# A new order of one block, new bank tables and a new list for the first blocks, in a fused causal convolution and SiLU MLP kernel

## The chip, the cores and the metric

The kernel runs on one core of one Trainium2 chip. The metric is the device time of one execution in microseconds (us); lower is better. Everything is float32.

## What is computed

A causal convolution over the sequence, with 7 taps per head that a softmax makes from `weight`, and behind it an MLP with SiLU:

```python
x_unf = x_pad[:, idx, :].reshape(B, S, K, H, group)   # B, S, D = 8, 4096, 192; K = 7, H = 8
out = np.einsum('hk,bskhg->bshg', softmax(weight), x_unf)
x = out.reshape(B * S, D)                             # 32768 tokens
h = x @ w_in                                          # 192 -> 2048
g = h * (1.0 / (1.0 + np.exp(-h)))
return g @ w_out                                      # 2048 -> 192
```

## The kernel before

The 32768 tokens are cut into 32 blocks of 1024, each in two parts of 512 tokens. Both matrix products are done with a fast scheme (as Strassen's and Winograd's): fewer products, and more sums of operands and of results around them. A block goes through these steps, each named by a short token in the kernel's text:

- **Convolution of the block to come.** `ld.k` loads x for channels k (k = 0, 1, 2) with 4 transfers on the sync queue (SP). `i.k` transposes it on VectorE. `v.ki` does tap i: tap 0 is a scaled copy on ScalarE into `nat`; taps 1 to 6 are done on VectorE (L516) for the first blocks, and from block 4 on are a scaled copy on ScalarE (L511) into a buffer `u`, and a transfer on GpSimd's queue (POOL) that adds it to `nat` (L512). `sp.k` spreads the result into `dup` on the SP queue (11 transfers a block, L533), `w.i` builds five sums of it (`win`, L550 and L553) on VectorE. `ha.0` fetches the 6 tokens from before the block.
- **Up phase** (tokens `P`, `L`; L649 and L666). `Pr.g` is product r (0 to 14) of group g (0 to 4): one matmul of 64 rows by 128 columns against 512 tokens. 64 rows are half of the TensorE array: a product is on rows 64 to 127 when r is in `ON_B` and (g, r) is not `SWAP`, otherwise on rows 0 to 63. The two halves can work at the same time. `L.0k` is one such matmul on rows 0 to 63, and `L.1k` one of 256 columns on each half. Products of one chain (`CHAINS`) add up in one PSUM bank. A block has 75 products P and 6 L: 40.5 full matmuls for each half.
- **Sums and SiLU of the results**: `u` copies a chain's bank to SBUF (ScalarE, L698), `X`, `a` and `b` add chains (VectorE, L692), `S` and `SL` apply SiLU (ScalarE, L710 and L715) into `g`. A product of another group can use a bank only when these have read it.
- **Output phase**: `t.ji` makes sums of `g` on VectorE (L733). `Di.je` (out_slot, L765) is four matmuls of 32 columns each, side by side in the array; 48 of them a block, 8 with 128 tokens (D5) and 40 with 512. They add up in the banks of `ACC`.
- **Results**: `x`, `y`, `z` copies (ScalarE), `M1` to `M7` sums (VectorE), `o.k` transposes, `st.k` stores 3 transfers each on the SP queue.

What order this runs in is written out by hand. `PLAN` is one string of tokens, and it is done once for each block b; a token with `-` ahead of it works on block b - 1, with `=` on b - 2, with `+` on b + 1. So one pass of the list does the output phase of the block before, while the convolution of the next is prepared, and then the up phase of block b; the list is a ring, and its last products are followed by the first tokens of the next pass (before: `... P8.2 b1.3 P4.3 P14.3`, and then `P5.0 -a1.3 -P10.2 ...`). `START` is a list of the same kind for the first blocks; in it `=dp` is a step of the plain second product of block 0 (`down_plain`, L786), whose banks are `DOWN_BANKS`, and `go.2` and combinations on GpSimd prepare the weights. Every instruction of the list is pinned to the program's order on its engine: each engine works its own queue in the order of the tokens, and waits on semaphores for the others.

The tables `CHAIN_BANKS`, `XBANKS`, `PLAIN_BANKS` and `ACC` say which of the 8 PSUM banks each chain and sum uses, one row for block 1, one for block 2 and one for all later blocks.

The end (`finish`) does the last block's second half and stores it.

Of the kernel before, what the change touches and what calls it, by code (L numbers as in the profile page):

```python
# [17 lines left out]
def kernel(  # L18
# [60 lines left out]


    PLAN = (
# [20 lines left out]
    )  # L102
    START = (
# [40 lines left out]
    )  # L144
    QUEUE = (0, 4, 1, 2, 3)
    CHAIN_BANKS = (
# [3 lines left out]
    )  # L150
    XBANKS = (
# [3 lines left out]
    )  # L155
    PLAIN_BANKS = (
        (0, 2, 3),
        (2, 2, 1),
        (6, 5, 7),
    )  # L160
    ACC = (
        (3, 2, 5, 6, 7, 1, 0),
        (4, 6, 3, 5, 1, 7, 0),
        (4, 7, 5, 1, 3, 6, 0),
    )

    def pin(ins):
        return tc.keep_in_program_order(ins)
# [37 lines left out]
    x0 = x.flatten_outer_dims()[TB - pad : TB, :].rearrange("t (k c) -> c k t", k=NK)  # L206
# [565 lines left out]
                )  # L772
            )

    DOWN_BANKS = (7, 4, 2)

    def down_plain(b):

        cmbs[b] = [xpool.tile([P, 4, TB], F32, tag="cmb", name="cmb")]
        for j in range(NJ):  # L780
            for a in range(2):
                for e in range(2):
                    for k in range(NK):
                        for n in range(2):
                            pin(
                                nc.tensor.matmul(  # L786
                                    banks[DOWN_BANKS[k]][R * n : R * n + R, :],
                                    wo[j][:, a, e, R * k : R * k + R],
# [14 lines left out]
    def copy_plain(b, k):  # L803
        pin(nc.scalar.copy(cmbs[b][0][:, k, :], banks[DOWN_BANKS[k]]))

# [329 lines left out]
```

## Time and profile before

| | us |
|---|---|
| runs of the kernel | 2368.7, 2369.21, 2367.38 |
| their median | 2368.7 |
| the profiled execution's own time | 2367.17 |
| its span (first to last instruction) | 2365.1 |

| part of the span | us |
|---|---|
| until the output phase of block 2 begins | 218.60 |
| 28 blocks of the planned order, to the output phase that begins at | 2250.14 |
| from there to the end | 114.96 |

How to read the profile: an engine's busy time is the time in which at least one of its instructions runs. PE is TensorE's matmuls, PEld its weight loads, DVE VectorE, ACT ScalarE, POOL GpSimd, SP the sync engine, and a q behind a name is its queue of transfers. Two matmuls on the two halves of the array overlap, and count once. The end of a matmul is modelled; its start is measured, so distances between starts are what can be trusted. L765 is line 765 of the kernel. The mean granted clock of TensorE is 0.999, so the clock was not held back.

Instructions of a group with their mean length (ns): a product (L649) is listed as two matmuls, one for each of the two passes in which a float32 matmul is done, of 589 to 595 each; the sums of L692 take 684 to 692 and those of L733 1219 to 1224; a copy of L698 587, SiLU 597 to 629, a scaled copy of L511 717.

### The profile page before, as it was taken

What the parts mean: (1) busy time and instruction counts of PE and PEld (TensorE: products, weight loads), DVE (VectorE), ACT (ScalarE), POOL (GpSimd) and SP (SyncE); (2) the same over time, 40 slices, a digit from 0 to 9 for tenths busy, and PEclk for the clock granted to TensorE, in tenths of its full rate; (3) what the DMA queues carried; (4) which work ended last, traced back from release to release, by engine and by line L of the source; (5) the groups of instructions that cost most, each with busy time, mean ns of one, the idle gap of its engine ahead of it and who ended that gap; (6) DMA issues with size and microseconds to landing.
All of it is one profiled execution on the core that took longest, in us unless ns stands there. A gap on an engine that the chain in (4) does not pass through costs nothing.

```text
span 2365.1 us, 45608 instructions
## 1 busy us (share of the span) xinstructions
PE 2352.3 (99%) x17630; PEld 1156.1 (49%) x17630; DVE 1797.8 (76%) x2373; ACT 1503.1 (64%) x2779; POOL 530.3 (22%) x672
## 2 busy tenths in 40 slices
PE   9999999999999999999999999999999999999998
PEld 5345544455544555444555445554445544455544
DVE  8898777787777777777877777777777777787776
ACT  5247666677666686666766666766667666677643
POOL 4921122211222111222122221212211122212100
PEclk9999999999999999999999999999999999999999
DMA  7324567665566655766656766556666567655510
GB/s 157 70 48 82 87 116 120 108 104 102 100 117 120 107 104 90 120 120 105 106 97 104 120 112 106 104 92 116 121 110 109 88 113 120 111 103 97 90 29 14
DMA packets 523833, 238.81 MB, mean 101 GB/s; under 512 B 431648, under 2 KB 436768, under 8 KB 523616
## 3 DMA queue, kind: packets, MB, share of 16 engines
q0 software_dynamic: 73024, 133.73, 33.4%
q1 hardware_dynamic: 447392, 101.78, 24.1%
q8 instruction: 138, 2.26, 0.4%
q10 hardware_dynamic: 3200, 0.39, 0.1%
q14 instruction: 79, 0.65, 0.1%
HBM read 31.46 MB, written 25.17 MB: 24 GB/s over the span
## 4 chain that ended last, share of the span: by engine, by line
PE 97%; DVE 2%; issue 0%; SPq 0%; ACT 0%; DMA 0%; DVEq 0%; ACTq 0%
PE ps L765 47%; PE ps L649 45%; PE ps L666 2%; PE ps L588 2%; DVE nat L516 1%; PE ps L1034 1%; DVE two L175 0%; DVE g L692 0%; PE ps L435 0%; DVE mh L175 0%; SPq L533 0%; DVE xt L477 0%; DVE t L733 0%; DMA dup<-nat 0%; DVE ps L692 0%
## 5 line engine op out<-in xcount | busy, mean ns | idle before, releaser
L512 POOL DMA_DIRECT2D nat<-u x504 | 431.7, 943 | 1586.4 <-DMA out_dram<-osb 716.0
L765 PE MATMUL ps<-g,wo 128*32 128x512 f32 x2976 | 681.1, 593 | 0.0
L649 PE MATMUL ps<-win,wr 64*128 64x512 f32 x1550 | 648.2, 594 | 0.0
L649 PE MATMUL ps<-win,ws 64*128 64x512 f32 x1550 | 617.7, 595 | 0.2 <-DVE ps L692 0.2
L698 ACT COPY u<-ps 128x512 f32<-128x512 f32 x775 | 444.0, 587 | 135.3 <-PE ps L649 115.5
L765 PE MATMUL ps<-t,wo 128*32 128x512 f32 (+1 forms) x4528 | 523.5, 446 | 0.0
L765 PE MATMUL ps<-t,wx 128*32 128x512 f32 x2976 | 475.1, 592 | 0.6 <-DVE t L733 0.6
L649 PE MATMUL ps<-dup,wr 64*128 64x512 f32 x868 | 442.6, 591 | 4.6 <-DVE ps L692 4.6
L692 DVE TENSOR_TENSOR g<-u,ps 128x512 f32<-128x512 f32 x465 | 315.3, 684 | 92.8 <-PE ps L649 63.4
L733 DVE TENSOR_TENSOR t<-g,t 128x1024 f32<-128x1024 f32 x248 | 303.4, 1224 | 105.6 <-PE ps L765 98.2
L710 ACT ACTIVATE g<-g 128x512 f32<-128x512 f32 x465 | 279.7, 629 | 139.9 <-DVE g L692 139.7
L733 DVE TENSOR_TENSOR t<-g 128x1024 f32<-128x1024 f32 x248 | 302.1, 1219 | 63.8 <-PE ps L765 58.1
L511 ACT ACTIVATE u<-xt,taps 128x512 f32<-128x512 f32 x504 | 341.7, 717 | 1.5
L649 PEld LDWEIGHTS ps<-win,wr 64*128 64x128 f32 x1550 | 262.8, 187 | 154.4 <-issue 71.3
L710 ACT ACTIVATE g<-ps 128x512 f32<-128x512 f32 x465 | 268.1, 597 | 73.7 <-PE ps L649 71.8
L649 PEld LDWEIGHTS ps<-win,ws 64*128 64x128 f32 x1550 | 264.6, 187 | 99.0 <-issue 34.3
L765 PEld LDWEIGHTS ps<-t,wo 128*32 128x32 f32 x4528 | 180.1, 110 | 220.3 <-issue 209.7
L649 PE MATMUL ps<-dup,ws 64*128 64x512 f32 x682 | 273.2, 594 | 0.0
L823 ACT COPY yx<-ps 32x128 f32<-32x128 f32 x120 | 30.8, 257 | 364.5 <-PE ps L765 363.1
L765 PEld LDWEIGHTS ps<-t,wx 128*32 128x32 f32 x2976 | 121.7, 110 | 278.4 <-issue 250.6
L765 PE MATMUL ps<-g,wx 128*32 128x512 f32 x1488 | 245.3, 592 | 0.0
L692 DVE TENSOR_TENSOR ps<-u,ps 128x512 f32<-128x512 f32 x310 | 214.3, 692 | 39.9 <-PE ps L649 24.3
(92 smaller groups left out, 2041.8 us busy)
## 6 DMA issues: line engine op xcount, KB each, us to landing
nat<-u POOLq DMA_DIRECT2D x504, 256.0 KB, 4.2
dup<-nat SPq DMA_DIRECT2D x345, 128.0 KB, 2.4
nat<-in_x_dram SPq DMA_DIRECT2D x382, 64.0 KB, 4.1
out_dram<-osb SPq DMA_DIRECT2D x376, 64.0 KB, 2.2
raw<-in_moe_w_out_dram SPq DMA_DIRECT2D x8, 384.0 KB, 3.7
raw<-in_moe_w_in_dram SPq DMA_DIRECT2D x12, 192.0 KB, 4.5
ws<-wr POOLq DMA_DIRECT2D x8, 192.0 KB, 4.9
raw<-in_moe_w_in_dram SPq DMA_DIRECT2D x6, 128.0 KB, 3.2
```

The lines of the kernel that those rows point to most:

```text
L511: pin(nc.scalar.activation(z, src, AF.Copy, scale=tap))
L512: pin(nc.gpsimd.dma_start(out=dst, in_=z, accum_op=ALU.add))
L516: nc.vector.scalar_tensor_tensor(out=dst, in0=src, scalar=tap, in1=dst, op0=ALU.mult, op1=ALU.add)
L588: nc.tensor.matmul(hs[a, n, e], rows(wr[j], e)[:, a, k, :], rows(d, e)[:, n, k, :], start=k == 0, stop=k == NK - 1,)
L649: nc.tensor.matmul(to[:, cols], raw(g, *LEFT[e][r], e), rhs[:, cols], start=first, stop=True, skip_group_check=True,)
L666: nc.tensor.matmul(plain_bank(b, n and 1 + e)[:, cols], rows(wr[j] if own == e else ws[j], e)[:, a, k, :], rows(dups[b], e)[:, SLOT[e][2 * ...
L692: pin(nc.vector.tensor_tensor(out_, u, v, op=op))
L698: pin(nc.scalar.copy(us[b, g, o][:, cols], t1[:, cols]))
L710: pin(nc.scalar.activation(h, src, AF.Silu))
L733: pin(nc.vector.tensor_tensor(t[i // 2][:, i % 2, :], u, v, op=ALU.subtract))
L765: nc.tensor.matmul(accs[b][at][SQ * q : SQ * q + SQ, to], lhs[:, e, SQ * k : SQ * k + SQ], rhs[:, e, ts(q, TB // 4) if i == 5 else to], st ...
L823: nc.scalar.copy(to[:, ts(q, TB // 4)], acc[5][SQ * q : SQ * q + SQ, 0 : TB // 4])
```

## The change

The lists PLAN and START and the tables of banks are replaced; no other line is changed but the banks of `down_plain`. The tokens of PLAN are the same ones, each once, in another order, and some are done one pass earlier or later (another sign). The functions that they call are the same. In START all steps `=dp` come ahead of the first product. Of START, the diff shows the lines that matter below.

```diff
     PLAN = (
-        "P5.0 -a1.3 -P10.2 -a0.2 -P10.3 -b5.3 -P8.3 -S4.3 -sp.0 -D0.31 -S0.1 -S1.0 -D1.10 v.20 "
-        "-S3.3 -D1.30 -S1.4 -D1.21 -D0.00 -t.00 -t.01 -D2.00 -D2.01 =st.1 v.11 -t.03 -D4.01 "
-        "-S1.1 -t.10 -D4.00 -D5.00 v.00 v.01 -D0.10 -sp.2 -t.11 -D2.10 -D1.01 v.12 -b5.2 v.02 "
-        "-t.13 -D5.10 -D4.10 -t.12 -D3.10 -D4.11 -S5.2 v.21 -w.0 -t.02 -D3.00 v.03 -D2.11 v.13 "
-        "-D3.01 -D1.11 -D5.11 -w.1 -D5.01 +ld.2 -D1.31 v.14 v.04 -D0.11 -D3.11 -D1.20 -a0.3 "
-        "v.15 u5.0 -S1.2 -S0.2 -t.20 -D0.20 -t.21 -D2.21 -t.22 -S0.3 -D2.20 -w.2 v.22 -S1.3 "
-        "+ld.1 -S5.3 -t.23 -D4.20 -D4.21 -D5.21 -D5.20 -D3.20 v.05 -t.30 -t.31 -D1.00 -t.33 "
-        "-D2.31 -D5.31 -D5.30 -x2.2 -x2.0 v.23 -D0.30 -D0.21 -D0.01 -y0.0 v.06 -t.32 -z1.0 v.24 "
-        "+ld.0 -D2.30 -w.3 -y1.0 -D3.21 -x2.3 -x2.1 -M1.0 -w.5 -D3.30 v.25 -D3.31 -x0.0 -D4.30 "
-        "-D4.31 -y2.0 P2.0 -x1.0 -w.4 -M2.0 u4.0 -M6.0 P5.4 u5.4 P3.0 L.00 -M3.0 -M4.0 L.11 "
-        "v.16 P6.0 -M5.0 -M7.0 L.02 u2.0 P2.4 u4.4 X2.0 v.26 L.12 -o.3 L.10 SL.1 SL.2 +i.0 P1.0 "
-        "u0.0 L.01 SL.0 P6.4 u2.4 P13.0 -o.0 S2.0 -o.2 P9.0 P5.1 P3.4 X4.0 P0.0 u1.0 X2.4 P12.0 "
-        "P11.0 P7.0 S4.0 b1.0 a5.0 P1.4 P14.0 -st.2 P13.4 u5.1 +i.2 P10.0 u0.4 S3.0 b5.0 P4.0 "
-        "a1.0 P2.1 -st.3 P9.4 S2.4 u4.1 P3.1 P0.4 u1.4 P12.4 P8.0 P5.2 u5.2 P6.1 X4.4 P7.4 -o.1 "
-        "b1.4 P14.4 P11.4 P10.4 u2.1 a0.0 S3.4 S4.4 a5.4 P2.2 u4.2 P4.4 X2.1 P13.1 S2.1 b5.4 "
-        "P9.1 a1.4 +i.1 P1.1 X4.1 P6.2 P3.2 u0.1 P8.4 a0.4 u2.2 X2.2 P5.3 P0.1 u5.3 P7.1 +ha.0 "
-        "P11.1 S0.0 P12.1 P2.3 P9.2 a5.1 P4.1 P13.2 u1.1 b1.1 P10.1 P1.2 a1.1 +v.10 S4.1 u4.3 "
-        "sp.1 S2.2 X4.2 b5.1 u0.2 P6.3 u2.3 P3.3 S5.1 X2.3 S0.4 P14.1 P8.1 a0.1 P11.2 S4.2 P7.2 "
-        "P0.2 S3.1 a5.2 u1.2 P9.3 X4.3 P12.2 P1.3 P4.2 S5.0 a1.2 u0.3 b1.2 P13.3 S2.3 P7.3 a5.3 "
-        "P14.2 S3.2 P0.3 u1.3 P12.3 S5.4 -st.0 P11.3 P8.2 b1.3 P4.3 P14.3"
+        "+ld.1 -P14.3 -S3.3 -sp.0 -S4.3 P5.0 -P8.2 v.00 v.01 -a1.3 -S1.3 -S1.2 -b5.3 v.20 -t.00 "
+        "-P8.3 -a0.3 -t.02 P5.4 -S0.1 -D1.20 -sp.2 -D1.21 -S5.1 -t.01 -t.03 u5.0 -D1.10 -D0.31 "
+        "-D1.31 v.21 -D2.01 -D1.00 -a0.2 -D3.00 -D3.01 -D2.00 u5.4 -D4.00 -D5.00 v.10 v.11 "
+        "-t.10 v.02 -D4.01 -D0.01 -D1.11 -S0.2 -D0.20 v.22 v.12 v.13 -t.11 -D2.10 -t.13 -D0.21 "
+        "-t.12 -D3.11 v.23 -D4.10 -D3.10 -D5.01 -w.0 v.24 -S5.2 v.03 -D5.10 v.25 -D2.11 -D0.11 "
+        "-D4.11 -D5.11 -S0.3 -t.20 -t.21 -D2.21 -D1.01 -D0.10 -t.23 -D4.20 v.04 v.14 -t.22 v.05 "
+        "-D0.30 v.15 -D2.20 -S5.3 -D1.30 -y1.0 -w.1 -D4.21 -t.30 -t.31 -t.32 -D3.21 -D0.00 "
+        "-D2.30 -D2.31 -y2.0 -t.33 -D5.30 -z1.0 -D3.31 -D3.20 v.06 -D5.21 -y0.0 -D5.31 -D5.20 "
+        "-x2.1 -x2.3 -x2.2 -x2.0 -D3.30 -x0.0 -M1.0 -M2.0 -D4.30 -D4.31 -x1.0 -w.2 -w.3 P2.0 "
+        "u4.0 -M3.0 +ld.2 P2.4 u4.4 -w.4 -M4.0 v.16 -M5.0 L.00 L.01 L.12 P6.0 P3.0 L.10 -M6.0 "
+        "-o.0 u2.0 L.11 SL.1 SL.2 P5.1 u5.1 L.02 P1.0 SL.0 X2.0 -w.5 +i.1 P9.0 u0.0 P13.0 S2.0 "
+        "P6.4 X4.0 u2.4 P3.4 P2.1 u4.1 P11.0 S4.0 X2.4 P7.0 a5.0 P0.0 +ld.0 u1.0 -st.0 P12.0 "
+        "b1.0 P9.4 X4.4 P1.4 P4.0 u0.4 a1.0 P13.4 -o.1 S2.4 -M7.0 P14.0 S3.0 P10.0 b5.0 P7.4 "
+        "a5.4 P0.4 u1.4 P6.1 u2.1 v.26 P8.0 a0.0 S5.0 P11.4 S4.4 P3.1 X2.1 P14.4 S3.4 P5.2 u5.2 "
+        "P1.1 u0.1 P12.4 b1.4 -o.3 -st.3 P13.1 S2.1 S0.0 P4.4 a1.4 S1.4 P5.3 P9.1 X4.1 P0.1 "
+        "+i.2 P12.1 P10.4 P2.2 b5.4 u5.3 u1.1 u4.2 P11.1 P7.1 b1.1 a5.1 S4.1 P8.4 a0.4 S1.0 "
+        "P2.3 u4.3 P6.2 u2.2 P3.2 X2.2 P4.1 a1.1 P10.1 S5.4 b5.1 P14.1 S3.1 sp.1 P3.3 P6.3 u2.3 "
+        "P9.2 P8.1 P1.2 P13.2 X4.2 X2.3 P1.3 P9.3 P11.2 -st.1 P7.2 a0.1 u0.2 +i.0 +ha.0 P0.2 "
+        "u0.3 P0.3 S2.2 P12.2 S4.2 u1.2 X4.3 P11.3 a5.2 P7.3 b1.2 -o.2 -st.2 a5.3 P14.2 P12.3 "
+        "u1.3 b1.3 P4.2 S3.2 P10.2 P13.3 S2.3 a1.2 P4.3 S0.4 b5.2 S1.1 P10.3"
     )
     START = (
-        "=dp.0 =v.00 -ld.2 =v.01 =v.02 =v.20 =v.21 =v.03 =v.04 =v.05 =v.06 =dp.1 =dp.2 =dp.3 "
...
-        "-ha.0 =go.2 -v.20 =dp.37 =dp.38 =sp.2 =w.0 =dp.39 =dp.40 =dp.41 =dp.42 -P5.0 -v.00 "
-        "=dp.43 =dp.44 -v.10 -v.11 -v.12 =w.1 ld.2 =w.2 =w.3 -u5.0 =dp.45 =cp.0 -v.01 -v.13 "
-        "=dp.46 =dp.47 =cp.2 -v.21 -v.22 -P2.0 -u4.0 -P5.4 -u5.4 -L.00 -v.02 -v.03 =cp.1 -v.23 "
...
-        "-w.1 -D4.10 -w.2 -P8.3 -S0.2 P2.0 -D4.11 +ld.0 -t.20 -D5.10 -D3.10 -t.21 -t.23 -D0.00 "
...
+        "-ld.1 =v.20 =v.21 =v.22 =v.23 =dp.0 =v.10 =v.11 =dp.1 =dp.2 =dp.3 =v.24 =dp.4 =v.00 "
...
+        "=dp.46 =dp.47 =cp.2 -P5.0 =cp.1 =o.1 -P5.4 -v.23 -v.24 -v.12 -u5.0 -P2.0 -P3.0 -u5.4 "
...
+        "-D3.30 -x0.0 P3.4 v.13 v.14 -w.5 P2.0 u4.0 P2.4 -M2.0 P3.0 P6.0 L.01 L.02 u4.4 u2.0 "
...
     )
     QUEUE = (0, 4, 1, 2, 3)
     CHAIN_BANKS = (
-        ((1, 0, 1, 3, 6), (5, 7, 5, 4, 2), (3, 6, 6, 1, 4)),
-        ((0, 0, 3, 7, 4), (3, 1, 6, 2, 6), (1, 2, 5, 1, 5)),
-        ((0, 7, 0, 6, 2), (4, 1, 3, 2, 5), (6, 4, 1, 5, 3)),
+        ((1, 2, 4, 6, 6), (7, 0, 5, 1, 0), (6, 7, 7, 4, 5)),
+        ((2, 6, 5, 4, 0), (4, 0, 6, 1, 3), (1, 2, 3, 0, 7)),
+        ((5, 2, 5, 6, 7), (0, 4, 0, 3, 3), (1, 7, 1, 2, 0)),
     )
     XBANKS = (
-        ((7, 3, 2, 2, 4), (7, 5, 0, 7, 4)),
-        ((5, 4, 4, 0, 5), (7, 5, 5, 4, 7)),
-        ((3, 4, 5, 4, 3), (1, 2, 5, 7, 6)),
+        ((2, 1, 3, 4, 3), (3, 4, 3, 3, 2)),
+        ((1, 3, 3, 7, 5), (7, 3, 7, 2, 5)),
+        ((4, 1, 1, 7, 4), (6, 1, 2, 4, 6)),
     )
     PLAIN_BANKS = (
-        (0, 2, 3),
-        (2, 2, 1),
-        (6, 5, 7),
+        (3, 4, 5),
+        (7, 2, 1),
+        (6, 1, 3),
     )
     ACC = (
-        (3, 2, 5, 6, 7, 1, 0),
-        (4, 6, 3, 5, 1, 7, 0),
-        (4, 7, 5, 1, 3, 6, 0),
+        (3, 6, 4, 1, 5, 7, 5),
+        (0, 3, 1, 2, 4, 6, 5),
+        (6, 2, 3, 1, 4, 0, 5),
     )
 
     def pin(ins):
@@ -772,7 +773,7 @@
                 )
             )
 
-    DOWN_BANKS = (7, 4, 2)
+    DOWN_BANKS = (7, 0, 2)
 
     def down_plain(b):
 
```

73 rows, old and new, of the table START are left out of this document.

## The prediction

> **What bounds the kernel now.** I read the page's busy times and its chain first, then the chain in order of time, then TensorE's timeline inside one block.
>
> ```profile
> PE 2352.3 (99%) x17630; PEld 1156.1 (49%) x17630; DVE 1797.8 (76%) x2373; ACT 1503.1 (64%) x2779; POOL 530.3 (22%) x672
> ...
> PE 97%; DVE 2%; issue 0%; SPq 0%; ACT 0%; DMA 0%; DVEq 0%; ACTq 0%
> ```
>
> TensorE is the bound, and 99% busy hides what is lost: L649's matmuls use half of the array, so "busy" also holds time in which one half stands still. The chain in order of time (start, length, what) repeats itself:
>
> ```profile
> 363.94 36.22 PE ps L765 x384
> 405.62 30.87 PE ps L649 x139
> 436.48 36.22 PE ps L765 x384
> ```
>
> A block takes 436.48 - 363.94 = 72.54 us: 36.22 in out_slot (L765) and 36.32 in the up phase (L649, L666). Starts at 218.60 and 2250.14 are 28 such blocks apart (28 x 72.55).
>
> Every matmul appears twice in TensorE's timeline, as two passes. Call array rows 0 to 63 half A and rows 64 to 127 half B; a product P(r.g) is on B when r is in ON_B and (g, r) is not SWAP.
>
> ```profile
> 413.18 0.59 PE L649 MATMUL ps<-win,ws 64*128 64x512 f32 x1
> 413.50 0.59 PE L649 MATMUL ps<-dup,wr 64*128 64x512 f32 x1
> 413.61 0.59 PE L649 MATMUL ps<-win,ws 64*128 64x512 f32 x1
> 413.93 0.59 PE L649 MATMUL ps<-dup,wr 64*128 64x512 f32 x1
> 414.04 0.59 PE L649 MATMUL ps<-win,wr 64*128 64x512 f32 x1
> ```
>
> These are P12.4 on A (413.18, 413.61), P8.0 on A (from 414.04) and P5.2 on B (413.50, 413.93), in PLAN's order P12.4, P8.0, P5.2. Each half takes a pass each 0.429 us (half B: 40 passes from 404.92 to 422.09), 0.858 a product, 0.429 for L.1k's 256 columns. And P5.2 starts 0.54 us ahead of P8.0, which stands before it: a half may run ahead of the order. It can't run far ahead:
>
> ```profile
> 403.64 0.59 PE L666 MATMUL ps<-dup,ws 64*128 64x256 f32 x2
> 404.06 0.81 PE L666 MATMUL ps<-dup,wr 64*128 64x256 f32 x3
> 404.49 0.69 PE L666 MATMUL ps<-dup,ws 64*128 64x512 f32 x1
> ...
> 404.92 0.59 PE L649 MATMUL ps<-win,ws 64*128 64x512 f32 x1
> 405.03 0.59 PE L666 MATMUL ps<-dup,ws 64*128 64x512 f32 x1
> ```
>
> Half A ends its second 256-column pass (403.86) at 404.07. Its next is L.01, which in PLAN stands behind L.10's part on B (404.49, 404.70) and P1.0 (404.92). L.01 starts only when L.10's first pass on B has started, with two loads (P1.0's) passed over: 0.42 us idle, and 0.10 more because its load was not ready (0.69 long where others take 0.59; second pass 0.53 later, not 0.43). The same at the end of the phase, where P10.2 stands behind P14.3 and P5.0, both on B:
>
> ```profile
> 432.62 0.59 PE L649 MATMUL ps<-win,wr 64*128 64x512 f32 x1
> ...
> 433.64 1.13 PE L649 MATMUL ps<-dup,ws 64*128 64x512 f32 x4
> ...
> 435.47 1.02 PE L649 MATMUL ps<-win,wr 64*128 64x512 f32 x2
> 436.41 1.06 PE L765 MATMUL ps<-g,wo 128*32 128x512 f32 x8
> ```
>
> A is free at 432.62 + 0.43 = 433.05, P10.2 starts at 433.64 beside P14.3 and pays 0.11 for its load: 0.70. So I read: a half's load passes over at most two waiting loads, one whole matmul of the other half. One loss is of another kind, the weight loads' waits:
>
> ```profile
> 422.64 0.29 PEld L649 LDWEIGHTS ps<-win,ws 64*128 64x128 f32 x2 [0.37 <-DVE ps L692]
> 423.23 0.18 PEld L649 LDWEIGHTS ps<-win,ws 64*128 64x128 f32 x1 [0.29 <-DVE g L692]
> ```
>
> P9.2 (A) and P4.1 (B) wait for VectorE to free a bank: 0.13 us on A, 0.40 on B.
>
> Sum for half A: 40.5 products x 0.858 = 34.76; first load of the phase 0.10; L.01 0.52; P9.2 0.13; P10.2 0.70; 0.09 until the array changes to L765's tiles (435.90 to 436.41 is 0.52, not 0.43). Together 36.30, measured 36.32.
>
> **The change part by part.** No instruction that computes or moves data is added or taken away: both built programs have 8815 matmuls, 2373 instructions on VectorE, and 1194 and 514 transfers on SP's and POOL's queues, in another order. TensorE's queue gets 30 instructions more that only wait (118 to 148), one a block, at 0.05 us on its sequencer: hidden, for in a pass of 0.43 us the loads of both halves leave it free for longer.
>
> *Order of products in PLAN.* I wrote down, ahead of each product, how many matmuls the other half is ahead in PLAN's order. Before: up to 3 (P10.2), and 2 at P3.0, L.01, P13.0, P13.4, P9.4 and P10.3; the two that cost are L.01 and P10.2, since A then stays behind and the other leads shrink. After: 2 once, at L.00, the first of its half in the phase, where both halves start empty (P3.0 has that place before and starts with B, at 400.09, at no cost); elsewhere 1 or less, A and B nearly alternate. L.01's 0.52 and P10.2's 0.70 go. Each half still has 40.5 products.
>
> *Waits for banks, with the new tables.* The trace can't show them for the new order. Lower end 0 (none on the half that ends last), upper end 0.53 (both places of today, 0.13 + 0.40, on the same half). Below 0 is excluded, for 34.76 is the work itself. I take 0.1, near what A pays today (0.13): chain and X banks are again reused only after other chains of the same or the next group. Behind a waiting load the queue holds the other half's too, so a wait would cost both.
>
> *Output phase.* 48 slots before and after; 36.22 stays. The t's and g's that they read are made in the same line of blocks; VectorE is 76% and ScalarE 64% busy, so both catch up within the block.
>
> *DMA steps moved.* SP's queue issues per block 12 loads (ld), 11 spreads, 12 stores and 2 small ones, some 37 x 0.55 us = 20 of 72.5; moving ld, sp, st past one another there delays each by a few us. In PLAN's own time (0.86 a slot, 0.43 a product) ld to i is 9 to 31 us before and 18 to 43 after, against 4.1 us to land; the last tap's addition to sp is 22 to 40 before and 22 to 36 after, against 4.2. Cost nothing, covered by these distances; uncovered, one late spread would cost its 2.4 us once a block. POOL's queue has 18 additions into nat a block; an addition behind one of the same k holds the queue for a landing. Such neighbours are v.13 v.14 and v.24 v.25 before, v.12 v.13 and v.23 v.24 after: two and two, so nothing.
>
> *START.* After, all of down_plain comes ahead of the first product, and the output phase of the first planned block isn't interrupted (before, P8.3 and P2.0 stand in it at 160.21). That saves two changes of tiles, 2 x 0.19 (0.10 + 0.09). The rest of the head hangs on VectorE's taps (L516), the same number in another order: from -3 (the holds that blocks 1 and 2 pay now, as above) to +3 (a late tap or spread: DMA dup<-nat 2.4). I take -1.
>
> Sum per block: 34.76 + 0.10 + 0.09 + 0.1 = 35.05 for 36.32, so 1.27 less. 28 x 1.27 = 35.6, with START 36.6: span 2365.1 - 36.6 = 2328.5. The profiled execution took 2367.17, 2.1 more than its span: 2330.6. The median of the runs is 1.5 above that execution: 2332.
>
> **Rivals.**
>
> *Waits take the place of the holds.* Nearly alternating halves run as fast as they can, so products come up to 1.2 us earlier relative to VectorE's and ScalarE's additions and copies. For: two loads already wait for DVE. Against: the idle time of both engines. With the upper end (0.53) twice a block, 1.06 - 0.1 more: 27 us, 2359; from half of that, 2345. 10%.
>
> *Matmuls start strictly in the queue's order.* Then the leads are not what costs. Walking PLAN so that none starts before the one ahead, an up phase would take 47.2 before and 45.7 after, so 1.5 less a block: 28 x 1.5 + 1 = 43, 2326. Against: 47.2 is far from 36.3, and P5.2 starts before P8.0. 2%. [...]
>
> *It doesn't do what it says.* The holds have another cause and come back elsewhere: 2365 to 2371. Against: both starts fall on the other half's pass to within 0.01 us. 3%.
>
> *POOL's additions become the bound: slower.*
>
> ```profile
> POOL nat L512 <- DMA out_dram<-osb: 716.0, 24, 31.1
> ...
> POOL nat L512 <- DMA nat<-u: 312.3, 120, 4.8
> ...
> nat<-u POOLq DMA_DIRECT2D x504, 256.0 KB, 4.2
> ```
>
> For: POOL already waits 11 us a block for landings (312.3 / 28), and one tap's addition must land before the next of its k. Against: 716 / 28 = 25.6 us a block of its idle time ends on old stores, so it has room. It decides from 25.6 / 18 = 1.4 us more per landing (4.2 to 5.6); beyond, each 0.1 us costs 18 x 0.1 = 1.8 a block. At 5.72 the loss is 2.2 a block, 0.9 more than the gain: 2369 + 25 = 2394. 5%.
>
> **How the numbers follow.** Forecast 80% (2326 to 2340 by the bounds of waits and START), waits 10%, strict starts 2%, no effect 3%, POOL 5%. The range 2326 to 2344 leaves out most of the waits, no effect and POOL, under 2 in 10. Faster by over 0.2% (some 5 us, what a measurement of this kernel can tell) 0.92, within 0.03, slower 0.05.
>
> **What would show it.** Blocks 71.2 to 71.4 us apart in the chain in order of time, L765's part still 36.2; in the up phase no 0.69 passes but its first and any that a load's wait explains; both halves ending within 0.1 us of each other. Wrong if the period stays above 72, if loads wait for DVE or ACT by more than 0.5 a block, or if the page's chain names POOL or DMA.

## The result, and the profile after

The changed kernel takes 2326.4 us (median of 4 runs, 2325.06 to 2327.43) where the kernel before takes 2368.7: a ratio of 0.9822, interval 0.9805 to 0.9839, so 1.8% faster. Its profiled execution took 2326.81, with a span of 2325.1 (before: 2367.17 and 2365.1). The forecast was 2332, its range 2326 to 2344.

The page of the changed kernel, busy times and the shares of the chain of waits:

```profile
PE 2315.7 (100%) x17630; PEld 978.7 (42%) x17630; DVE 1776.7 (76%) x2373; ACT 1505.4 (65%) x2779; POOL 535.9 (23%) x672
...
PE 99%; DVE 0%; ACT 0%; issue 0%; ACTq 0%
```

The counts are those of before. TensorE is busy 36.6 us less (2352.3 before): most of the 40.0 us that left was inside its "busy". POOL, SP's queue and landings of transfers do not stand in the chain; ScalarE's queue (ACTq) has under half a per cent of it.

The chain in order of time (start, length, what):

```profile
211.52 36.22 PE ps L766 x384
...
354.17 36.22 PE ps L766 x384
395.33 30.11 PE ps L650 x139
425.44 36.22 PE ps L766 x384
```

All lines of the kernel's text moved down by one (L766 is out_slot, L650 and L667 the up phase). Blocks are 425.44 - 354.17 = 71.27 us apart, with 36.22 in out_slot as before. Over all steady blocks the median distance between first matmuls of output phases is 71.263 (before 72.546), of which the up phase is 35.045 (before 36.328). A few blocks take 0.02 to 0.29 us more, so on the mean a block gains 1.265, against 1.283 by the medians.

TensorE's timeline at the start and at the end of that up phase (start, length of one, engine, line, operation):

```profile
390.32 0.69 PE L650 MATMUL ps<-win,wr 64*128 64x512 f32 x1
390.33 0.69 PE L667 MATMUL ps<-dup,ws 64*128 64x512 f32 x1
...
390.87 0.59 PE L667 MATMUL ps<-dup,ws 64*128 64x512 f32 x1
...
391.30 0.59 PE L667 MATMUL ps<-dup,ws 64*128 64x512 f32 x1
...
415.75 0.67 PE L650 MATMUL ps<-win,ws 64*128 64x512 f32 x1
...
424.81 0.59 PE L650 MATMUL ps<-win,wr 64*128 64x512 f32 x1
424.85 0.59 PE L650 MATMUL ps<-dup,wr 64*128 64x512 f32 x1
425.37 0.63 PE L766 MATMUL ps<-g,wx 128*32 128x512 f32 x3
```

L.00 (390.33, 390.87) is followed by L.01 at 391.30, one pass of 0.43 later: no hold. Between the first passes (0.69) and the end one pass is clearly longer than 0.59, by 0.08, at 415.75. Both halves start their last pass within 0.04 of each other.

Where the 40.0 us of span went, by the first matmuls of output phases:

| stretch | before | after | difference | forecast |
|---|---|---|---|---|
| start to the second output phase | 218.53 | 211.45 | -7.1 | -1 |
| from there to the last output phase | 2103.39 | 2067.08 | -36.3 | -35.6 |
| last output phase to the end | 43.19 | 46.58 | +3.4 | 0 |
| span | 2365.1 | 2325.1 | -40.0 | -36.6 |

So the blocks are as forecast, and two terms at the ends were mis-sized in opposite directions. (The second stretch has 29 blocks, one more than the forecast counted: the first of them gains 1.54 and the last 0.62.) The experiments take them one after the other.

### The profile page after: what moved, and what is told of

Its sections match the earlier page's. It is cut to its first block, busy times and chain, and to the rows that moved or that the text cites. A ratio compares the mean times of both kernels' runs of the same rounds, so it can differ in the third digit from the quotient of the medians.

```text
span 2325.1 us, 45494 instructions
## 1 busy us (share of the span) xinstructions
PE 2315.7 (100%) x17630; PEld 978.7 (42%) x17630; DVE 1776.7 (76%) x2373; ACT 1505.4 (65%) x2779; POOL 535.9 (23%) x672
## 4 chain that ended last, share of the span: by engine, by line
PE 99%; DVE 0%; ACT 0%; issue 0%; ACTq 0%
PE ps L766 48%; PE ps L650 45%; PE ps L667 2%; PE ps L787 2%; PE ps L589 2%; PE ps L1035 1%; PE ps L436 0%; DVE t L734 0%; DVE g L693 0%; DVE cmb L176 0%; ACT u L176 0%; DVE osb L176 0%; PE ps L462 0%; DVE zeros L176 0%; ACTq L969 0%
## 5 line engine op out<-in xcount | busy, mean ns | idle before, releaser
L650 PE MATMUL ps<-win,wr 64*128 64x512 f32 x1550 | 716.3, 591 | 0.0
L766 PE MATMUL ps<-g,wo 128*32 128x512 f32 x2976 | 677.1, 593 | 0.0
L650 PE MATMUL ps<-win,ws 64*128 64x512 f32 x1550 | 636.9, 592 | 0.0
L766 PE MATMUL ps<-t,wo 128*32 128x128 f32 (+2 forms) x4528 | 518.2, 447 | 0.0
L699 ACT COPY u<-ps 128x512 f32<-128x512 f32 x775 | 442.2, 589 | 117.1 <-PE ps L650 87.6
L766 PE MATMUL ps<-t,wx 128*32 128x512 f32 x2976 | 495.4, 592 | 2.2 <-DVE t L734 2.2
L512 ACT ACTIVATE u<-xt,taps 128x512 f32<-128x512 f32 x504 | 347.1, 724 | 166.1 <-DMA nat<-u 165.6
L650 PE MATMUL ps<-dup,wr 64*128 64x512 f32 x868 | 422.5, 590 | 0.0
L650 PEld LDWEIGHTS ps<-win,wr 64*128 64x128 f32 x1550 | 284.8, 187 | 201.6 <-issue 179.0
L650 PEld LDWEIGHTS ps<-win,ws 64*128 64x128 f32 x1550 | 264.2, 186 | 163.9 <-issue 93.8
L693 DVE TENSOR_TENSOR g<-u,ps 128x512 f32<-128x512 f32 x465 | 309.3, 676 | 5.6 <-PE ps L650 5.3
L829 ACT COPY yx<-ps 32x512 f32<-32x512 f32 x150 | 86.9, 579 | 296.3 <-PE ps L766 294.9
L650 PE MATMUL ps<-dup,ws 64*128 64x512 f32 x682 | 269.8, 590 | 0.0
L766 PEld LDWEIGHTS ps<-t,wo 128*32 128x32 f32 x4528 | 179.6, 110 | 204.5 <-issue 201.3
L766 PE MATMUL ps<-g,wx 128*32 128x512 f32 x1488 | 246.6, 595 | 0.0
L766 PEld LDWEIGHTS ps<-g,wo 128*32 128x32 f32 x2976 | 170.9, 110 | 148.5 <-issue 139.1
```

The costliest lines, as they stand in the source:

```text
L512: pin(nc.scalar.activation(z, src, AF.Copy, scale=tap))
L650: nc.tensor.matmul(to[:, cols], raw(g, *LEFT[e][r], e), rhs[:, cols], start=first, stop=True, skip_group_check=True,)
L693: pin(nc.vector.tensor_tensor(out_, u, v, op=op))
L699: pin(nc.scalar.copy(us[b, g, o][:, cols], t1[:, cols]))
L766: nc.tensor.matmul(accs[b][at][SQ * q : SQ * q + SQ, to], lhs[:, e, SQ * k : SQ * k + SQ], rhs[:, e, ts(q, TB // 4) if i == 5 else to], st ...
L829: pin(nc.scalar.copy(to, acc[3 * (name[0] == "x") + k][n:P, :]))
```

## The experiments

Spans are those of the profiled execution of each kernel; "first output phase" is its first matmul in TensorE's timeline. Times are medians, ratios are to the kernel before, run on the same chip.

### Do two moved products give the blocks' gain?

Three runs change nothing of before but the place of one or two products in PLAN. L.01 ahead of P1.0:

```diff
-... L.12 -o.3 L.10 SL.1 SL.2 +i.0 P1.0 u0.0 L.01 SL.0 ...
+... L.12 -o.3 L.10 SL.1 SL.2 +i.0 L.01 P1.0 u0.0 SL.0 ...
```

> The kernel before, with L.01 alone moved ahead of P1.0 in PLAN (tables, first blocks and everything else as before). By the window of two waiting loads, half A no longer stands behind P1.0's two loads: the hold of 0.52 goes, less up to 0.10 that one of the places with a lead of 2 may take back. Period of a block 72.55 - 0.42 = 72.13, span 2365 - 28 x 0.42 = 2353 (2350 to 2356). Rival, matmuls start strictly in the queue's order: the walk gives the up phase 0.21 more, period 72.76, span 2371. Rival, holds have another cause: no change, 2365.

Measured: period 72.15, 0.40 less a block; span 2355.2; 2357.6 us, ratio 0.9955 (0.994 to 0.997).

P10.2 ahead of P5.0, so that its lead falls from 3 to 2:

```diff
-"P5.0 -a1.3 -P10.2 -a0.2 -P10.3 ...
+"-P10.2 P5.0 -a1.3 -a0.2 -P10.3 ...
```

> The kernel before, with P10.2 alone moved ahead of P5.0 at the head of PLAN. By the window of two loads only P14.3 stands ahead of it, the lead falls from 3 to 2: the hold of 0.70 falls to 0 to 0.10. Period 72.55 - 0.65 = 71.90 (71.85 to 71.95), span 2365 - 28 x 0.65 = 2347 (2345 to 2349). Strict order of starts: the walk gives 0.86 less a block, period 71.69, span 2341. Another cause: no change.

Measured: period 71.85, 0.70 less, so this lead of 2 cost nothing; span 2346.6; 2348.6 us, ratio 0.9918 (0.9903 to 0.9933).

Both moves:

> The kernel before with both moves (L.01 ahead of P1.0, P10.2 ahead of P5.0), bank tables and first blocks as before. Window of two loads: both gains add up, 1.05 to 1.20 a block, period 71.35 to 71.50, span 2365 - 28 x 1.12 = 2334 (2331 to 2336); so two products moved do nearly all of what the new order does for a block, and new tables and the moved DMA steps are worth 0.1 to 0.2 a block at most. Strict order: 0.65 less a block, period 71.90, span 2347. If the gain hangs on the new bank tables: no change, 2365.

Measured: period 71.42, 1.13 less; span 2335.2; 2337.2 us, ratio 0.987 (0.9855 to 0.9884). TensorE's timeline of this kernel, at L.01:

```profile
402.75 0.38 PE L666 MATMUL ps<-dup,wr 64*128 64x256 f32 x1
402.77 0.68 PE L666 MATMUL ps<-dup,ws 64*128 64x512 f32 x1
```

L.01 (402.77) now starts beside the first pass of L.12's part on half B (402.75), with the two loads of L.10's part on B still waiting ahead of it, and pays 0.10 for a load that was not ready: that is why it gives 0.40 and not 0.52. In time this is a lead of 1, two matmuls of 256 columns; in loads it is four, as many as a lead of 2. What follows: two moved products, with the old tables and the old first blocks, give 1.13 of the new order's 1.28 a block. Strict order of starts is refuted: it wanted the first of these runs slower, and the third at 71.90. So is "the gain hangs on the new tables". Of the 0.16 left, most is what remains in this kernel's up phase, that 0.10 and a pass of 0.69 at VectorE's wait near P9.2 (420.92), against 0.08 in the changed kernel. The new order with the old tables was not tried.

### Where is the limit?

Two runs put a lead back into the changed kernel, at one place. P10.3 (half A) behind P14.3 and P5.0 of half B, a lead of 2:

```diff
-"+ld.1 -P14.3 -S3.3 -sp.0 -S4.3 P5.0 -P8.2 ...
+"+ld.1 -P14.3 -S3.3 -sp.0 -S4.3 P5.0 -P10.3 -P8.2 ...
...
-... P4.3 S0.4 b5.2 S1.1 P10.3"
+... P4.3 S0.4 b5.2 S1.1"
```

> The changed kernel with P10.3 alone moved back in PLAN, behind P14.3 and P5.0 of half B: half A then meets a lead of 2 (P10.3's place has 0 in the changed kernel). Window of two waiting loads: when A is free, P14.3's first pass starts, so the loads still ahead of P10.3's are P5.0's two; it passes over both and pays only for a load that is not ready, 0 to 0.11. Period 71.26 + 0.10 = 71.36 (71.26 to 71.37), span 2325 + 28 x 0.10 = 2328. Strict order of starts: the walk gives 0.86 more, period 72.12, span 2349. No limit at all: no change.

Measured: period 71.373, 0.110 more; span 2329.1; 2329.6 us, ratio 0.9835 (0.9821 to 0.985).

The same with P5.4 ahead of P10.3 too, a lead of 3:

```diff
-"+ld.1 -P14.3 -S3.3 -sp.0 -S4.3 P5.0 -P8.2 ... -P8.3 -a0.3 -t.02 P5.4 ...
+"+ld.1 -P14.3 -S3.3 -sp.0 -S4.3 P5.0 P5.4 -P10.3 -P8.2 ... -P8.3 -a0.3 -t.02 ...
```

> As the run with a lead of 2, and P5.4 of half B moved ahead of P10.3 too, so that the lead is 3. Window of two waiting loads: P10.3 has to wait until two more passes of B have started, 0.86, and its load is not ready, 0.10: 0.96 a block more than in the changed kernel; period 72.22, span 2325 + 28 x 0.96 = 2352 (2350 to 2354). The step from a lead of 2 to a lead of 3 should be some 9 times the step from 0 to 2. Strict order: the walk gives 1.28, period 72.54, span 2361. No limit: no change.

Measured: period 72.231, 0.968 more; span 2352.1; 2353.8 us, ratio 0.9937 (0.992 to 0.9953). TensorE's timeline of this run, where the hold is:

```profile
424.29 0.59 PE L650 MATMUL ps<-dup,wr 64*128 64x512 f32 x1
424.32 0.59 PE L650 MATMUL ps<-win,ws 64*128 64x512 f32 x1
424.75 1.02 PE L650 MATMUL ps<-dup,ws 64*128 64x512 f32 x2
425.61 0.59 PE L650 MATMUL ps<-dup,wr 64*128 64x512 f32 x1
425.62 0.69 PE L650 MATMUL ps<-dup,ws 64*128 64x512 f32 x1
```

Half A starts its last pass of P13.3 at 424.29 and is free at 424.72. P14.3's two passes on B run from 424.75 and P5.0 starts at 425.61; P10.3 starts 0.01 after it (425.62), with P5.4's two loads still waiting ahead of it, and its first pass is 0.69 long. The loads of this stretch:

```profile
424.75 0.19 PEld L650 LDWEIGHTS ps<-dup,ws 64*128 64x128 f32 x1 [0.24 <-issue]
425.18 0.19 PEld L650 LDWEIGHTS ps<-dup,wr 64*128 64x128 f32 x1 [0.24 <-issue]
425.61 0.19 PEld L650 LDWEIGHTS ps<-dup,wr 64*128 64x128 f32 x1 [0.24 <-issue]
425.61 0.29 PEld L650 LDWEIGHTS ps<-dup,ws 64*128 64x128 f32 x2
```

When P5.0's first load runs (425.18), three loads of half B still wait ahead of P10.3's (P5.0's second and P5.4's two), and P10.3's stays behind, though half A is free; when P5.0's second runs (425.61), two are left, and P10.3's goes with it. So the step from a lead of 2 to a lead of 3 costs 0.858, two passes, and a lead of 2 only the 0.11 of a late load. That is the window of two loads read from the trace of before, in its sizes; "no limit" (no change in either run) and "strict order" (0.86 and 1.28 more) both fail.

### The finish

In the changed kernel TensorE stands still at the beginning of the last output phase. Its timeline there (in brackets: idle time ahead of it, and what ended it):

```profile
2281.78 0.63 PE L766 MATMUL ps<-t,wx 128*32 128x512 f32 x3 [2.19 <-DVE t L734]
...
2282.66 0.77 PE L766 MATMUL ps<-g,wx 128*32 128x512 f32 x3
...
2283.19 1.09 PE L766 MATMUL ps<-g,wx 128*32 128x512 f32 x3
...
2284.05 3.07 PE L766 MATMUL ps<-t,wo 128*32 128x256 f32 x32
```

and the stretches of 5 us (length, then busy time of PE, PEld, DVE, ACT, POOL with counts, then the granted clock, DMA share, GB/s):

```profile
2278.00:2283.00 5.00, 2.81 (x22) 0.57 (x24) 4.90 (x6) 2.74 (x6) 0.00 (x0) 1.00 0.00 0
2283.00:2288.00 5.00, 5.00 (x52) 2.18 (x48) 3.01 (x4) 2.19 (x4) 0.00 (x0) 0.66 0.00 0
```

In the last block the slots of the held half (j of 2 and 3) are left out, so PLAN's order there is D1.10, D2.01, and D2.01 reads a t that VectorE makes until 2281.7. After the wait the passes are 0.53 and 0.86 apart (2282.66, 2283.19, 2284.05) instead of 0.43, at a granted clock of 0.66 in the stretch: it is 0.50 from 2282.98 to 2286.39, for 3.41 us. In the kernel before the wait was 0.60, and the clock stayed at 1.00:

```profile
2324.44 0.63 PE L765 MATMUL ps<-t,wx 128*32 128x512 f32 x3 [0.60 <-DVE t L733]
```

So the finish lost 2.19 - 0.60 = 1.59 by waiting, and the other 1.80 of the 3.39 fits 3.41 us at half clock (1.71 lost). The run puts two slots that need no t in between:

```diff
-"-D1.31 v.21 -D2.01 -D1.00 -a0.2 ... -D4.01 -D0.01 -D1.11 ...
+"-D1.31 v.21 -D1.00 -D0.01 -D2.01 -a0.2 ... -D4.01 -D1.11 ...
```

> The changed kernel with D1.00 and D0.01, which read only g, moved ahead of D2.01, which reads a t. In the last block, where the slots of the held half are left out, D2.01 is the second slot and TensorE stands still 2.19 us for VectorE's t (2279.6 to 2281.78 in the profile of the changed kernel), and its passes are then 0.5 to 0.9 apart instead of 0.43 until 2284.9. Theory: two slots of 0.86 cover 1.72 of it, 0.5 is left as in the kernel before, and the clock stays: from the last output phase's start to the end 46.58 becomes 43.2 (43.0 to 44.0), time 2326.4 - 3.3 = 2323 (2322 to 2324.5); blocks stay at 71.26. Rival: the slow passes come from something else in this place (a transfer, the weights' loads): only 1.7 less, 44.9. Or VectorE is late for the next slot as well: no change.

Measured: blocks 71.263 as in the changed kernel, the last stretch 44.04 instead of 46.58, span 2322.9; 2324.7 us (2324.31 to 2324.73, against 2325.06 to 2327.43 of the changed kernel), ratio 0.9814 (0.98 to 0.9829). Its stretches:

```profile
2278.00:2283.00 5.00, 4.54 (x35) 1.09 (x36) 4.89 (x6) 3.11 (x7) 0.00 (x0) 1.00 0.00 0
2283.00:2288.00 5.00, 5.00 (x71) 2.37 (x68) 3.55 (x5) 2.19 (x4) 0.00 (x0) 1.00 0.00 0
```

The clock stays, and of the wait 0.46 is left, both as the theory said; a new wait of 0.35 for the next t (at 2290.24) takes some back, so the end comes just outside the 43.0 to 44.0 expected. Of the 2.54 gained, 2.19 - 0.46 - 0.35 = 1.38 is waiting. The other 1.16 is a remainder, put down to the clock; 3.41 us at half clock would be 1.71, so some 0.5 is paid elsewhere in this order, and where was not resolved. This is the fastest version of the study.

### The head

Before, TensorE stands still in the first row phase too. Its timeline, VectorE's, and the stretches, all of the kernel before:

```profile
107.86 0.59 PE L666 MATMUL ps<-dup,ws 64*128 64x512 f32 x1
113.07 0.69 PE L649 MATMUL ps<-dup,wr 64*128 64x512 f32 x1 [4.62 <-DVE ps L692]
```

```profile
98.23 0.69 DVE L550 TENSOR_TENSOR win<-dup 128x512 f32<-128x512 f32 x1 [5.55 <-DMA dup<-nat]
...
103.18 7.84 DVE L516 SCALAR_TENSOR_TENSOR nat<-xt,taps,nat 128x512 f32<-128x512 f32 x9
```

```profile
107.00:112.00 5.00, 1.45 (x9) 0.59 (x5) 4.93 (x7) 1.98 (x5) 4.85 (x8) 1.00 0.01 2
112.00:117.00 5.00, 3.93 (x11) 2.16 (x13) 3.83 (x6) 1.66 (x3) 4.63 (x9) 0.67 0.34 52
```

TensorE waits 4.62 us for X2.0 on VectorE (112.33), which stands behind nine taps in a row, a transpose and one more tap; the granted clock then is 0.67, which the mean of 0.999 over the span doesn't show. VectorE itself had waited 5.55 us for a spread. The changed kernel has neither; its stretches:

```profile
107.00:112.00 5.00, 5.00 (x30) 3.24 (x28) 4.70 (x7) 3.42 (x7) 4.69 (x9) 1.00 0.08 14
112.00:117.00 5.00, 5.00 (x26) 2.44 (x24) 4.70 (x8) 3.93 (x9) 4.63 (x10) 1.00 0.72 113
```

First output phase: 145.04 before, 139.76 after (kernels with the START of before: 145.0 to 146.7). Part of that spread goes with the clock: in the kernel before it is at half for 3.41 us (113.74 to 117.16), and its mean over the span is 0.999; in the three runs with moved products, whose START is the same, the mean is 0.998, which is an estimate of 5 to 10 us at half (less the 1.0 us of clock that the kernel before loses at its end), and these begin the phase at 146.1 to 146.7. So a change of about 1 us in this number means little unless the slow stretches are equally long. Four runs looked for the one place that does it, and none found it. First the taps, behind X2.0:

```diff
-... -v.02 -v.03 =cp.1 -v.23 -P3.0 -L.10 -v.04 -v.05 ld.0 -P6.0 -u2.0 =o.2 -P2.4 ...
-"-v.24 ld.1 -X2.0 =o.1 -L.01 ... -P1.0 -u0.0 =w.4 -P13.0 ...
+... -v.02 -v.03 =cp.1 -P3.0 -L.10 ld.0 -P6.0 -u2.0 -P2.4 ...
+"ld.1 -X2.0 =o.2 -v.23 -v.04 =o.1 -L.01 ... -P1.0 -u0.0 -v.05 -v.24 =w.4 -P13.0 ...
```

> The kernel before, PLAN and tables as before; in START four taps of VectorE (v.23, v.04, v.05, v.24) and one transpose (o.2) stand behind X2.0 instead of ahead of it. Theory: TensorE's idle 4.6 us at 108.45 of the profile before ends on X2.0 (112.33), which waits in VectorE's queue behind these; 4 x 0.86 + 0.62 = 4.1 us sooner leaves at most 0.6 of idle time, and the granted clock (0.67 in 112 to 117 us, passes 0.85 apart instead of 0.43) stays at 1.00, which is worth another 1.6: first output phase from 145.0 to 139.5 (139 to 141), span 2365 - 5.5 = 2359.5 (2358 to 2361). Rival: the taps that come later make the next stage late, and the stall moves on: 2364 to 2366.

Measured: first output phase 146.15, span 2366.1, ratio 0.9996 (0.9986 to 1.0005). TensorE's idle time in this kernel's timeline:

```profile
109.53 0.69 PE L649 MATMUL ps<-dup,wr 64*128 64x512 f32 x1 [1.03 <-DVE ps L692]
...
116.35 2.08 PE L649 MATMUL ps<-win,wr 64*128 64x512 f32 x4 [3.12 <-DVE ps L692]
```

The rival was right: the wait for X2.0 fell to 1.03, and 3.12 came back behind the next two X, with the clock at 0.81 and 0.51 in the two stretches from 112 on. Next, the spread that VectorE waits for:

```diff
-... =v.24 =v.25 =v.26 -ld.0 ... =dp.38 =sp.2 =w.0 ...
+... =v.24 =v.25 =v.26 =sp.2 -ld.0 ... =dp.38 =w.0 ...
```

> The kernel before with one thing moved in START: sp.2, the last spread of the first planned block on SP's queue, stands right behind the tap that it needs (v.26) instead of behind sp.1, i.1, i.0 and ha.0. In the run with the taps moved the stall only moved on, so VectorE has too much to do there; before, it stood idle 5.55 us until 98.23 for the landing of sp.2 (issued 95.19 to 97.7). Theory: that wait starts the head's loss. With sp.2 early, only sp.1 (91.36 to 93.74, and 2.4 to land) is waited for: VectorE goes on at 95.5 to 96, X2.0 and TensorE's restart come 2.2 to 2.7 sooner; the first output phase from 145.0 to 146.7 (what the kernels with this START showed) to 142 to 144, up to 1.6 less still if the clock stays up. Rival: the head's loss lies in the first products' order: 145 to 147, no change.

Measured: first output phase 150.01, ratio 1.0014 (1.0004 to 1.0023), worse: loads behind the spread on SP's queue came late, and VectorE waited 5.55 for them (97.22) and 3.23 for ScalarE's first tap (102.60). The place was wrong, so once more, behind the loads:

```diff
-... -ld.1 =dp.31 =dp.32 =v.16 =sp.1 ... =dp.38 =sp.2 =w.0 ...
+... -ld.1 =dp.31 =dp.32 =sp.2 =v.16 =sp.1 ... =dp.38 =w.0 ...
```

> The kernel before with sp.2 moved in START again, now behind the loads ld.0 and ld.1 and ahead of v.16 and sp.1 (in the run before it stood ahead of ld.0, so the loads waited behind it on SP's queue and VectorE's 5.55 us of idle time only changed its cause, from DMA dup<-nat to DMA nat<-in_x_dram, with 3.23 more behind it). Theory: VectorE's idle time ahead of w.0 ends with sp.1's landing at 95.5 to 96 instead of 98.2, so X2.0 and TensorE's restart come 2.2 to 2.7 sooner: first output phase 142 to 144.5 instead of 145.0 to 146.7, span 2362 to 2363. Rival: VectorE isn't what holds the head, 145 to 147.

Measured: first output phase 144.55, ratio 0.9991 (0.9982 to 1.0001). VectorE waited 1.65 for the spread and then 2.59 for ScalarE's first tap (L508): 4.24 instead of 5.55, and TensorE's wait fell from 4.62 to 3.37. And both edits together:

> Both changes of START together: sp.2 behind the loads and ahead of sp.1, and the four taps and the transpose behind X2.0. Theory, VectorE has too much work ahead of the first products because it stood idle before: with 2.2 to 2.7 us of that back, the two stalls of the run with the taps moved (1.03 and 3.12) shrink to at most 1.5 in sum and the clock stays at 1.00: first output phase 140 to 142, span 2359 to 2361. Rival: something else, not VectorE's work, ends the second stall: 143 to 146.

Measured: first output phase 144.84, ratio 0.9989 (0.9979 to 0.9998). X2.0 came at 107.46 (before 112.33), but TensorE still waited 3.00 for the next X (114.14), since VectorE was busy from 102.28 to 115.4 without a break. The clock was 0.70 and 0.62 here in the two stretches from 112 on, and 0.81 and 0.51 with the taps moved: by an estimate from these shares, 6.8 us at half in both. With the spread behind the loads it was 0.66 in the first of them and 1.00 in the next, 3.4 us at half. Compared at about equal length, the taps alone gave nothing (146.15 against 146.1 to 146.7), the spread alone 0.5 (144.55 against 145.04), and both 1.3 to 1.9 of the 5.3 looked for. So the theory fell in its size: neither the late spread nor the taps' places are the whole of it. What is left is a reading, which no run isolates: how much of VectorE's work stands in the first row phase. In the kernel before, 24 taps and none of the sums `win` start ahead of the first product (97.00); in the changed kernel 28 taps and five sums do (101.55), and from 90 to 100 us VectorE is busy 9.4 us instead of 4.4.

The last run asks whether the head's gain is START's at all. It has the START and the first tables of the changed kernel (with five tokens at its end that the next order needs done), and PLAN and the tables' last rows of before. Where the two orders meet, at blocks 2 and 3, their bank tables differ, so the numbers that come out are other ones; no instruction that computes or moves data is left out.

```diff
-        "+ld.1 -P14.3 -S3.3 -sp.0 -S4.3 P5.0 -P8.2 v.00 v.01 -a1.3 ...
+        "P5.0 -a1.3 -P10.2 -a0.2 -P10.3 -b5.3 -P8.3 -S4.3 -sp.0 ...
...
-"S4.2 P10.2 b5.2 P10.3 -st.2 S1.1"
+"S4.2 P10.2 b5.2 P14.3 P10.3 b5.3 P8.2 -st.2 S1.1 S5.1 +v.10"
...
-        ((5, 2, 5, 6, 7), (0, 4, 0, 3, 3), (1, 7, 1, 2, 0)),
+        ((0, 7, 0, 6, 2), (4, 1, 3, 2, 5), (6, 4, 1, 5, 3)),
...
```

> The changed kernel's START (with P14.3, P8.2, S5.1, v.10 and b5.3 added at its end, which the next order needs done) and its bank tables for blocks 1 and 2, but PLAN and the tables' last rows of the kernel before. Theory: the head's gain belongs to START alone, the blocks' gain and the loss at the finish to PLAN. So the first output phase starts at 139.2 to 139.8 and the second at 211.5 to 212.5 as in the changed kernel (145.04 and 218.53 before); blocks are 72.55 apart; from the last output phase to the end 43.2 as before (46.58 in the changed kernel). Span 2365.1 - 7.1 = 2358, later by what block 3 pays for meeting another order than the one it was laid out for (0 to 4.5): 2358 to 2362.5. Rival, the head's gain needs PLAN's new order too (part of it is paid back as soon as the old order sets in): 2363 to 2366.

Measured: output phases at 140.06 and 212.54 (0.26 and 0.04 above what was expected), blocks 72.546 apart, last stretch 43.19. The block at the seam took 76.57, 4.0 more; span 2363.2, 0.7 above the range and inside the rival's (2363 to 2366), 2364.0 us, ratio 0.9982 (0.9972 to 0.9992). So the head comes out 5.0 to 6.0 us earlier with START and the first tables alone, and the blocks' gain and the finish's loss belong to PLAN. But the rival is right in that 4.0 of these 6.0 are paid back where the old order sets in: a list of first blocks kept its gain only with the order that it leads into.

## Why the prediction was right, point by point

- **Two halves, and a window of two loads.** Right, and now shown: the lead of 2 was priced at 0.10 and cost 0.110, the lead of 3 at 0.96 and cost 0.968; two products moved give 0.40 and 0.70, and 1.13 together.
- **L.01's 0.52 and P10.2's 0.70 go.** P10.2's 0.70 was measured to 0.01, already at a lead of 2; so a lead of 2 costs 0 or 0.11 by where it falls. L.01's move alone gives 0.40; the other 0.10 goes only where L.12's and L.10's four loads on half B don't stand ahead of it either, as in the changed kernel.
- **Waits for banks, 0.1.** The size was right, the cause not: the one pass that is clearly late in the block shown (0.08, at 415.75) waited for ScalarE (u, L699), where the prediction named VectorE. Up phase 35.05 forecast, 35.045 measured; 1.27 a block forecast, 1.283 by the medians and 1.265 on the mean measured.
- **Output phase, DMA steps, POOL.** Nothing, as said: 36.217 before and after, and 4.2 us from issue to landing for the additions into nat, as before.
- **START, -1 within -3 to +3.** Mis-sized, and outside its bounds: -7.1. The step that failed is "the rest of the head hangs on VectorE's taps, the same number in another order". The same number of taps is not the same wait: TensorE stood still 4.62 us in the head of before for an X behind taps, that line was in the profile before, and it was not priced, nor the clock after it. -5.3 comes by the first output phase and -1.8 in the block behind it: 1.28 that every block gains, and 0.5 where the output phase is no longer interrupted (priced at 0.38). The holds of blocks 1 and 2 stood only in the bound of -3 and not in the -1. Which part of START's new order frees VectorE stays open.
- **The finish, no term.** Also mis-sized, by +3.4. A list that leaves tokens out in the last block is another list there; its second slot now was one that waits.
- **From the span to the median.** The execution took 1.7 more than its span (2.1 forecast), and the median of the runs is 0.4 below that execution (1.5 above forecast).

The forecast of 2332 missed 2326.4 by 5.6: 6.1 of head and 0.7 of blocks too little gained, 3.4 of finish not seen, 2.3 from the last point. So the time lies inside the range, at its lower end, and partly because two errors stand against each other: had the finish been as before, it would have come out at 2323, below the range.

**The rivals.** Strict order of starts gave 2326, the measured time, and is still wrong: it wanted 71.05 between blocks (71.263 measured), and the runs with one product moved went the other way or by another size. Waits in place of holds: one of 0.08. No effect, and POOL as the bound: refuted by the period and by the chain.

## What to carry to other kernels

Where two row tiles share one queue, count in program order how far one half's next load stands behind the other's: here a lead of one matmul was free, a lead of two cost 0 to 0.11 us, and the third cost its whole time (0.858), while the engine shows as busy. Price the head and the finish of a periodic program by their own timelines, for their waits are not those of the period; a list that skips tokens there must be read with these left out. And look for a wait of a few microseconds on TensorE before anything smaller, since here each of 2.19 to 4.62 us was paid twice, the second time as a granted clock of 0.51 to 0.81 in stretches of 5 us.

## What the runs showed of the hardware

**Idle time and the clock.** Waits of 0.46 (the run with two slots moved ahead), 0.60 (the kernel before, 2324.44) and 1.03 us (the run with the taps moved) left the granted clock at 1.00 in their stretches of 5 us. With waits of 2.19, 3.00, 3.12, 3.37 and 4.62 it fell to 0.51 to 0.81 in stretches of 5 us, with passes up to 0.86 apart where others are 0.43. Taken by itself the slow stretch has a clock of 0.50 and lasts 3.41 us behind the waits of 2.19 (2282.98 to 2286.39 in the changed kernel) and of 4.62 (113.74 to 117.16 in the kernel before). With those of 3.00 and 3.12 the shares give 6.8 us at half, the estimate above.

**How far loads are pulled ahead.** In these runs a load passed two waiting loads of the other half and no third one: in the run with a lead of 3 P10.3's stayed behind three at 425.18 and went past two at 425.61, and the step from a lead of 2 to a lead of 3 cost 0.858. At one place that tells loads from time it went by loads: L.01 was late by 0.10 behind four loads of two matmuls of half the columns (402.77, in the run with both moves).
